# A chunked linear recurrence with a cosine-gated second part: one written order for all engines, the back substitution between block transposes, weights in small steps

## The chip, the cores and the metric

The kernel runs on one core of a Trainium2 chip. The metric is the device time of one execution in microseconds, the median of several runs. The engines of the core are TensorE (PE, with PEld for its weight loads), VectorE (DVE), ScalarE (ACT), GpSimd (POOL) and SyncE (SP, which here only issues DMAs). Each works through its own queue in order and waits on semaphores for the others.

## The reference

```python
# r, k, v, w, a, b: (batch 4, heads 8, seq 768, dim 40) float32
state = zeros(B, H, D, D)
for t in range(S):
    y[:, :, t] = einsum('bhd,bhde->bhe', rt, state)
    Sa = einsum('bhde,bhe->bhd', state, at)
    state = state * wt[:, :, None, :] - einsum('bhd,bhe->bhde', Sa, bt) \
            + einsum('bhd,bhe->bhde', vt, kt)
x = y.transpose(0, 2, 1, 3).reshape(3072, 320)
h = x @ w_in            # 320 x 2048, float64 in memory
out = (h * cos(h)) @ w_out   # 2048 x 320, float64 in memory
```

## The kernel before

The sequence is cut into 24 chunks of 32 steps. All four batches and eight heads of a chunk are worked on at once. Inside a chunk the recurrence is a triangular system, so each chunk needs the inverse of a 32 x 32 triangular matrix per head and batch. One DVE back substitution (`inv_step`, 31 steps of two operations each) gives the inverses of four chunks together, 128 of them, one per partition.

The work comes in segments that each use one tile `at` of PSUM, a pool of two buffers:

- `p1_w`, `p1_a` (once per chunk), `p1_b`, `p1_n` prepare two chunks: transposes of `w` (PSUM tile `wT`), running products on DVE (`wp`), their reciprocals (`rw`), scaled `a` and `b`, and the triangular matrices `nt`. They reach the layout of the back substitution over DRAM (`nd`, then `u`), and the inverses come back over DRAM too (`rd`, then `rt`).
- `p2_v`, `p2_k`, `p2_g` prepare one chunk ahead (tiles `vT`, `kT`, `gram`).
- `ch_t`, `ch_q`, `ch_x`, `ch_s`, `ch_z` (tiles `sT`, `qps`, `x0ps`, `sps`, `dps`) carry the state through the chunk. `ch_z` takes both buffers of `at`. Its four additions into the state `qz` and four into `yt` run on DVE, the four decays of `qz` on POOL. `ch_t` of the next chunk transposes `qz`.
- `yt` goes to DRAM (`xd`) and comes back as token columns `xT`.

The second part takes two chunks as one token group `g` and the 2048 columns in four blocks `j`. Each of the 48 pairs is four pieces: `first_a` and `first_b` (PSUM tiles `ph`, one buffer pair, with the rounding, Abs and Sin on ACT and DVE that give `gT`), and two `second` pieces of the pair before (tiles `po`). That makes 192 pieces. They are strewn between the segments by the counter `due`, 7.71 to a chunk from chunk 2 on; a piece of group `g` is allowed from chunk `2g + 2`.

The weights are float64. `rounded` turns the words into float32 with five DVE and two ACT operations per block, its DMAs issued from the ACT queue.

PE's order is the written one (`manual_schedule(engines={PE})`). On DVE, ACT, POOL and SP a list scheduler sets the order, so that an operation can pass others that are written ahead of it.

Of the kernel before, what the change touches and what calls it, by code (L numbers as in the profile page):

```python
# [9 lines left out]
F32 = mybir.dt.float32  # L10
# [10 lines left out]
def kernel(  # L21
# [11 lines left out]
):  # L33

# [70 lines left out]
    nat = {n: kept(f"nat_{n}", [P, H, DP], 2, 1.0, padding, nc.vector) for n in "w"}  # L105
    nat |= {n: kept(f"nat_{n}", [P, H, DP], 2, 0.0, padding) for n in "ab"}
    nat |= {n: kept(f"nat_{n}", [P, H, D], 1) for n in "kvr"}
# [9 lines left out]
    def load(c, names, via=nc.sync):  # L117
        for n in names:
            for i in range(B):
                via.dma_start(  # L120
                    nat[n][c % len(nat[n])][blk[i], :, :D],
                    src[n][i, :, c * C : (c + 1) * C, :].rearrange("h t d -> t h d"),
                )

    load(0, "w")
    load(1, "w")
    load(0, "a", nc.scalar)
    load(1, "a", nc.scalar)
    load(0, "b")
    load(1, "b")  # L130


    ident = kept("ident", [P, P])[0]
    make_identity(nc, ident)
# [9 lines left out]
    w0 = kept("w0", [P, 4 * B, C], 1, 0.0, on=nc.vector)[0]  # L144
    w1 = kept("w1", [P, 4 * B, C], 1, 0.0, on=nc.vector)[0]
    bn_b = kept("bn", [P, H, DP], 7, 0.0, padding)
    kn_b = kept("kn", [P, H, DP], 2, 0.0, padding)

    w_in_sb = const.tile([P, 2, DFF], F32, tag="w_in", name="w_in_sb")
    w_in_tail = const.tile([P, NF // 4, 2, P], F32, tag="w_in_tail", name="w_in_tail")
    w_out_sb = const.tile([P, NF, DM], F32, tag="w_out", name="w_out_sb")
# [5 lines left out]
    def rounded(dst, src, by, by_sb):  # L159


        n, wid = dst.shape[0], dst.shape[-1]
        words = sb2.tile([P, 512, 2], I32, tag="gT", name="words")[:n, :wid]
        for rows, part in src:
            nc.scalar.dma_start(words[rows].rearrange("p n w -> p (n w)"), part.bitcast(I32))
        lo, hi = words[:, :, 0], words[:, :, 1]
        mant = sb3.tile([P, 512], I32, tag="turns", name="mant")[:n, :wid]
        expo = sb2.tile([P, 512], I32, tag="expo", name="expo")[:n, :wid]
        frac = mant.bitcast(F32)
        nc.vector.tensor_scalar(  # L170
            expo, hi, 20, 0x7FF, ALU.logical_shift_right, ALU.bitwise_and
        )
        nc.scalar.activation(expo, expo, ACTF.Relu, bias=to_bits[:n], scale=2.0**23)
        nc.vector.tensor_scalar(mant, hi, 0xFFFFF, None, ALU.bitwise_and)
# [489 lines left out]
```

## Time and profile before

| | us |
|---|---|
| median of 3 runs (1079.9 to 1084.45) | 1080.34 |
| profiled execution | 1084.64 |
| its span | 1082.9 |
| PE busy | 820.3 (76%) |
| PE weight loads busy | 628.6 (58%) |
| DVE busy | 505.2 (47%) |
| ACT busy | 355.8 (33%) |
| POOL busy | 179.0 (17%) |
| mean granted TensorE clock | 0.884 |

The 40 slices of the page show three stages: some 100 us in which DVE is the busy engine and PE hardly works, a long middle with PE at 70 to 90%, and a last stretch of some 60 us with PE at 90% and more. In the chain that ended last PE has 54% of the span, DVE 20%, ACT 11% and DMA 8%. The costliest groups are the matmuls into `po` (249.2 us) and `ph` (208.9 and 56.7 us).

### The profile page before, as it was taken

Reading aid. Unit: us, or ns where it says so; the run is one execution under the profiler, and the core shown is the slowest. Engines: PE = TensorE matmul, PEld = TensorE weight load, DVE = VectorE, ACT = ScalarE, POOL = GpSimd, SP = SyncE. Lnnn points to the kernel's source line nnn. Section 1 sums busy time; section 2 is a strip of 40 time slices with the busy share of each in tenths; the row PEclk is TensorE's granted clock in tenths of the full one; section 3 lists DMA queues with packets and bytes.
Section 4 is the critical chain, followed back from the end, with each engine's and each line's share of the span. In section 5 each row is a group of like instructions: output and inputs, shape, how many; then the busy total and the mean of one; then the engine's idle time right before and its main releaser. Section 6 shows DMA issues by size and latency. Waiting matters only on the chain.

```text
span 1082.9 us, 36890 instructions
## 1 busy us (share of the span) xinstructions
PE 820.3 (76%) x16472; PEld 628.6 (58%) x16472; DVE 505.2 (47%) x1112; ACT 355.8 (33%) x679; POOL 179.0 (17%) x352
## 2 busy tenths in 40 slices
PE   4221366856679698788879879878987979999998
PEld 3110355644567576566667667656766757667775
DVE  6888124484452465251557263385255383233221
ACT  2341111422423242322243343224432424234343
POOL 4110123011120201120211120212022021111000
PEclk9999995877798798887898889889899989899999
DMA  5662432325124223124223123223241223200000
GB/s 114 147 159 40 83 62 55 38 57 137 35 50 62 52 46 72 34 44 59 49 47 78 37 57 55 54 48 67 40 82 25 47 57 56 46 15 10 21 26 12
DMA packets 235518, 61.65 MB, mean 57 GB/s; under 512 B 209504, under 2 KB 229472, under 8 KB 235360
## 3 DMA queue, kind: packets, MB, share of 16 engines
q1 hardware_dynamic: 229088, 48.48, 24.8%
q10 hardware_dynamic: 6272, 10.82, 3.5%
q8 instruction: 129, 2.11, 0.8%
q14 instruction: 29, 0.24, 0.1%
HBM read 45.09 MB, written 14.16 MB: 55 GB/s over the span
## 4 chain that ended last, share of the span: by engine, by line
PE 54%; DVE 20%; ACT 11%; DMA 8%; issue 4%; POOL 2%; SPq 1%; ACTq 0%; DVEq 0%; POOLq 0%
PE ph L97 20%; PE po L97 16%; DVE inv_tmp L309 3%; DVE inv L313 3%; PE gram L97 3%; DMA words<-in_moe_w_in_dram 3%; DVE rw L251 3%; ACT turns L531 3%; DMA words<-in_moe_w_out_dram 3%; PE x0ps L97 3%; ACT turns L530 3%; DVE wp L235 2%; PE vT L216 2%; PE qps L97 2%; PE sT L386 2%
## 5 line engine op out<-in xcount | busy, mean ns | idle before, releaser
L97 PE MATMUL po<-w_out_sb,gT 128*128 128x320 f32 x768 | 249.2, 476 | 0.3 <-issue 0.3
L97 PE MATMUL ph<-xT,w_in_sb 128*128 128x256 f32 x768 | 208.9, 426 | 20.3 <-DVE w_in_sb L182 9.5
L97 PEld LDWEIGHTS po<-w_out_sb,gT 128*128 128x128 f32 x768 | 154.1, 209 | 67.9 <-issue 23.6
L97 PEld LDWEIGHTS ph<-xT,w_in_sb 128*128 128x128 f32 x768 | 160.3, 215 | 50.7 <-DVE w_in_sb L182 10.4
L529 DVE SCALAR_TENSOR_TENSOR turns<-turns,ph 128x512 f32<-128x512 f32 x96 | 61.6, 682 | 212.1 <-ACT turns L528 212.0
L528 ACT ACTIVATE turns<-ph,rnd 128x512 f32<-128x512 f32 x96 | 60.9, 684 | 176.8 <-PE ph L97 176.8
L532 DVE TENSOR_TENSOR gT<-ph,turns 128x512 f32<-128x512 f32 x96 | 65.8, 690 | 59.8 <-ACT turns L531 59.6
L309 DVE TENSOR_TENSOR inv_tmp<-u,inv 128x31 f32<-128x31 f32 (+15 forms) x186 | 69.2, 372 | 5.5
L313 DVE TENSOR_TENSOR inv<-inv,inv_tmp 128x31 f32<-128x31 f32 (+15 forms) x186 | 68.4, 368 | 5.7
L531 ACT ACTIVATE turns<-turns,half_pi 128x512 f32<-128x512 f32 x96 | 68.7, 723 | 1.8
L97 PE MATMUL gram<-aT,kT 40*32 40x32 f32 x1536 | 20.0, 222 | 64.8 <-DVE yt L482 49.6
L530 ACT ACTIVATE turns<-turns 128x512 f32<-128x512 f32 x96 | 59.3, 625 | 10.6 <-DVE turns L529 10.6
L97 PEld LDWEIGHTS gram<-aT,kT 40*32 40x32 f32 x1536 | 17.2, 124 | 69.4 <-issue 52.0
L97 PE MATMUL ph<-xT,w_in_tail 64*128 64x256 f32 x384 | 56.7, 415 | 0.0
L378 ACT COPY vvm<-gram 128x256 f32<-128x256 f32 x24 | 8.9, 372 | 137.9 <-DVE vvm L374 137.9
L251 DVE RECIPROCAL rw<-wn 128x320 f32<-128x320 f32 x24 | 51.5, 2148 | 5.0 <-PE wn L216 5.0
L476 POOL TENSOR_TENSOR qz<-qz,wc 128x160 f32<-128x160 f32 x92 | 40.0, 462 | 68.5 <-DVE qz L475 68.5
L328 POOL TENSOR_TENSOR kn<-nat_k,rw 128x320 f32<-128x320 f32 x24 | 21.2, 882 | 177.0 <-PE dps L97 170.1
L216 PE MATMUL bT<-ident,bn 128*128 128x128 f32 x96 | 22.4, 377 | 33.3 <-POOL bn L256 11.2
L264 ACT COPY bT<-bT 128x512 f32<-128x512 f32 x24 | 14.1, 586 | 101.5 <-PE bT L216 101.3
L239 POOL COPY wx<-wp 128x496 f32<-128x496 f32 x24 | 15.0, 626 | 193.2 <-DVE wp L235 190.8
L97 PEld LDWEIGHTS ph<-xT,w_in_tail 64*128 64x128 f32 x384 | 34.6, 195 | 20.0 <-issue 17.2
(93 smaller groups left out, 1096.9 us busy)
## 6 DMA issues: line engine op xcount, KB each, us to landing
words<-in_moe_w_out_dram ACTq DMA_DIRECT2D x16, 320.0 KB
words<-in_moe_w_in_dram ACTq DMA_DIRECT2D x8, 512.0 KB
nat_w<-in_w_dram SPq DMA_DIRECT2D x96, 40.0 KB
nat_b<-in_b_dram SPq DMA_DIRECT2D x96, 40.0 KB
nat_k<-in_k_dram SPq DMA_DIRECT2D x96, 40.0 KB
nat_v<-in_v_dram SPq DMA_DIRECT2D x96, 40.0 KB
nat_r<-in_r_dram SPq DMA_DIRECT2D x96, 40.0 KB
xd<-yt SPq DMA_DIRECT2D x48, 80.0 KB
```

Source lines behind the costliest of these rows:

```text
L97: nc.tensor.matmul(o, lhsT=lhsT, rhs=rhs, start=start, stop=stop, skip_group_check=True)
L216: nc.tensor.transpose(ps[:, i * P : (i + 1) * P], x[:, 2 * i : 2 * i + 2].rearrange("p e d -> p (e d)"), ident)
L235: nc.vector.tensor_tensor_scan(flat(wp), flat(w0), flat(w1), 0.0, ALU.mult, ALU.add)
L251: nc.vector.reciprocal(rw, unpad(ps[:, 0].rearrange("p (h d) -> p h d", h=H)))
L309: nc.vector.tensor_tensor(tmp, u[:, :j, j : j + 1].to_broadcast([P, j, C - j]), x[:, j : j + 1, j:].to_broadcast([P, j, C - j]), ALU.mult,)
L313: nc.vector.tensor_tensor(x[:, :j, j:], x[:, :j, j:], tmp, ALU.subtract)
L476: nc.gpsimd.tensor_tensor(z, z, wc.rearrange("p (f m b) -> p f m b", f=2, m=2)[:, :, :, bb] .unsqueeze(3).to_broadcast([P, 2, 2, D]), ALU. ...
L528: nc.scalar.activation(n, u, ACTF.Identity, bias=rnd, scale=1.0)
L529: nc.vector.scalar_tensor_tensor(n, n, -ROUND, u, ALU.add, ALU.subtract)
L530: nc.scalar.activation(n, n, ACTF.Abs)
L531: nc.scalar.activation(n, n, ACTF.Sin, bias=half_pi, scale=-2.0 * math.pi)
L532: nc.vector.tensor_tensor(G["gT", j][:, 2 * e : 2 * e + 2].rearrange("p f t -> p (f t)"), u, n, ALU.mult)
```

## The change

- `manual_schedule()` without engines: all engines follow the written order. The code hands out operations by hand for that: `later(n, work)` puts work n steps behind, `step` runs a segment or piece and then what has come due, and adds up to `of_inv` back substitution steps and `of_w` weight steps behind each segment or piece (1, in every fourth chunk 2, and 4 or 3).
- The order of segments within a chunk is new, one piece count of 8 per chunk from 2.4 on replaces 7.71 from 2 on.
- `nt` and the inverses go through DVE block transposes (`nc.vector.transpose`, 32 x 32) instead of DRAM. `inv_step` itself is unchanged. The 33 steps of one back substitution all lie in the chunk whose number is 3 modulo 4.
- The running product reads PSUM: the column copies `w0` on ACT go, a `memset` of every 32nd column in PSUM comes, and one tile `wb` replaces `wp` and `wx` (no POOL copy of 496 columns).
- The inputs of chunks 0 to 3 have landing places of their own at first; those of 2 and 3 lie in parts of `w_in_sb` and `w_out_sb` that the weights fill later. All are fetched at the start.
- Weights come in 36 blocks (28 before: `w_in` in halves of 256 columns), fetched from the POOL queue, three ahead, converted in chunks 0 to 3.
- `ph`'s products are issued one step after the rest of `first_b`.

```diff
-    w0 = kept("w0", [P, 4 * B, C], 1, 0.0, on=nc.vector)[0]
+    w1 = kept("w1", [P, 4 * B, C], 2, 0.0, on=nc.vector)
...
+        def fetch():
+            t["words"] = sb3.tile([P, DM, 2], I32, tag="words", name="words")[:n, :wid]
+            for rows, part in src:
+                nc.gpsimd.dma_start(
...
+    def step(work, of_inv=0, of_w=0):
+        before = list(waiting)
+        work()
+        for w in before:
+            w[0] -= 1
+            if w[0] == 0:
+                waiting.remove(w)
+                w[1]()
+        for steps, n in ((inv_steps, of_inv), (w_steps, of_w)):
+            for _ in range(min(n, len(steps))):
+                steps.pop(0)()
...
-            nc.scalar.copy(w0[:, :, 1:], b4(ps[:, i])[:, :, 1:])
...
+        nc.vector.memset(ps[:, :, ::C], 0.0)
+        for i in range(2):
+            wb = ring.tile([P, 4 * P + 1], F32, tag="wb", name="wb")
+            nc.vector.tensor_tensor_scan(wb[:, 1:], ps[:, i], flat(w1[i]), 0.0, ALU.mult, ALU.add)
...
-        nc.sync.dma_start(nd.rearrange("p h t -> p (h t)"), nt.rearrange("p c e n -> p (c e n)"))
...
+        nc.vector.transpose(
+            G["u"].rearrange("p (s t) -> p t s", s=C), G["nt"].rearrange("p h t -> p t h")
+        )
...
-        nc.sync.dma_start(rd.rearrange("p s t -> p (s t)"), G["inv"])
...
+        nc.vector.transpose(
+            rt.rearrange("p c h t -> p t (c h)"), G["inv"].rearrange("p (s t) -> p t s", s=C)
+        )
...
-    with tc.manual_schedule(engines={mybir.EngineType.PE}):
+    with tc.manual_schedule():
...
+        START, done = 2.4, 0
...
+            if c == 0:
+                segs = [x, v, extra[0], s, k, extra[1], z, g, *extra[2:]]
+            elif len(extra) == 3:
+                segs = [t, v, q, k, x, extra[0], s, g, z, *extra[1:]]
+            elif len(extra) == 2:
+                segs = [t, v, q, k, x, g, s, extra[0], z, extra[1]]
+            else:
+                segs = [t, v, q, k, x, g, s, z]
...
+            fill = (1 + (c % 4 == 3), 4 if c < 2 else 3)
+            for i, seg in enumerate(segs):
+                step(seg, *fill)
+                due = (c + (i + 1) / n - START) * 8
...
+                    step(pieces[done][1], *fill)
...
+                if c % 4 == 2 and len(extra) == 2 and seg is extra[1]:
+                    inv_steps.extend(inverse(q0))
```

On PE, around `ch_z` of a chunk in the middle. Before:

```order
L97 MATMUL sps<-x_6813,rt 32x72 x32
L216 MATMUL kT<-ident_128,kn_161 128x128 x4
L97 MATMUL ph<-xT,w_in_sb 128x256 x4
L97 MATMUL ph<-xT,w_in_tail 128x256 x4
L97 MATMUL dps<-vvm_101,kn_163 64x72 x32
L97 MATMUL dps<-sm,bn_155 64x72 x32
L97 MATMUL gram<-aT,kT 32x32 x32
L97 MATMUL gram<-rT,vT 32x32 x32
L97 MATMUL po<-w_out_sb,gT 128x320 x8
L386 MATMUL sT<-ident_128,qz_102 128x128 x8
```

After:

```order
L101 MATMUL gram<-aT,kT 32x32 x32
L101 MATMUL gram<-rT,vT 32x32 x32
L101 MATMUL po<-w_out_sb,gT 128x320 x4
L101 MATMUL sps<-x_5274,rt 32x72 x32
L101 MATMUL ph<-xT,w_in_sb 128x256 x4
L270 MATMUL bT<-ident_84,bn_202 128x128 x4
L270 MATMUL bT<-ident_84,bn_204 128x128 x4
L101 MATMUL ph<-xT,w_in_sb 128x256 x4
L101 MATMUL ph<-xT,w_in_tail 128x256 x4
L101 MATMUL dps<-vvm_114,kn_206 64x72 x32
L101 MATMUL dps<-sm,bn_194 64x72 x32
L101 MATMUL nps<-aT,bT 32x32 x64
```

`gram` no longer follows `dps`; it stands two segments ahead of it, and behind `dps` comes a `p1` segment or a piece.

On DVE, in a chunk that carries the back substitution (`inv_tmp`, `inv`). Before, where steps run in a row until an operation with a due time of its own comes:

```order
L309 TENSOR_TENSOR inv_tmp<-u,inv 128x135
L313 TENSOR_TENSOR inv<-inv,inv_tmp 128x27x5
L309 TENSOR_TENSOR inv_tmp<-u,inv 128x156
L313 TENSOR_TENSOR inv<-inv,inv_tmp 128x26x6
L427 COPY x_4232<-x0ps 128x288
L309 TENSOR_TENSOR inv_tmp<-u,inv 128x175
L313 TENSOR_TENSOR inv<-inv,inv_tmp 128x25x7
```

After, near the end of the fourth chunk:

```order
L560 TENSOR_TENSOR yt<-dps,qz_116 128x4x32
L381 TENSOR_TENSOR inv_tmp<-u,inv 128x112
L385 TENSOR_TENSOR inv<-inv,inv_tmp 128x4x28
L381 TENSOR_TENSOR inv_tmp<-u,inv 128x87
L385 TENSOR_TENSOR inv<-inv,inv_tmp 128x3x29
L616 SCALAR_TENSOR_TENSOR turns<-turns,ph 128x512 x2
L381 TENSOR_TENSOR inv_tmp<-u,inv 128x60
L385 TENSOR_TENSOR inv<-inv,inv_tmp 128x2x30
L381 TENSOR_TENSOR inv_tmp<-u,inv 128x31
L385 TENSOR_TENSOR inv<-inv,inv_tmp 128x31
L327 RECIPROCAL rw<-wn 128x320
L329 TENSOR_TENSOR aT<-wn,wb 128x512
```

Two steps (four operations) stand behind every segment and piece, in one chunk of four.

On SP, between the write of `xd` and the read of `xT`. Before:

```order
L493 DMA xd<-yt 40x4x128 x2
L120 DMA nat_b_91<-in_b_dram 32x8x40 x2
L500 DMA xT<-xd 128x2x128
L502 DMA xT<-xd 64x128 x2
L120 DMA nat_b_91<-in_b_dram 32x8x40
```

After:

```order
L574 DMA xd<-yt 40x4x128 x2
L149 DMA nat_k<-in_k_dram 32x8x40 x4
L149 DMA nat_v<-in_v_dram 32x8x40 x4
L149 DMA nat_r<-in_r_dram 32x8x40 x4
L584 DMA xT<-xd 128x2x128
L586 DMA xT<-xd 64x128 x2
```

Twelve loads of a coming chunk now stand between the two.

## Rows read from the trace of the kernel before

**Rows 1.** Stretches: bounds, length, busy us of the engines, clock, DMA share, GB/s.

```profile
core 0: us, PE busy (x) PEld busy (x) DVE busy (x) ACT busy (x) POOL busy (x), PEclk, DMA share, GB/s
921.25:1012.39 91.14, 84.50 (x1828) 64.58 (x1835) 25.52 (x62) 34.46 (x67) 12.21 (x21) 0.93 0.11 27
301.73:921.25 619.52, 522.81 (x10901) 400.57 (x10908) 292.89 (x642) 209.19 (x406) 113.57 (x211) 0.87 0.29 53
96.05:301.73 205.68, 123.75 (x2717) 96.68 (x2717) 92.56 (x219) 53.16 (x103) 33.41 (x62) 0.81 0.32 62
...
1012.39:1082.90 70.51, 65.18 (x584) 47.96 (x584) 19.04 (x33) 26.67 (x45) 1.27 (x1) 0.99 0.05 15
```

**Rows 2.** PE in order of time, around `gram` behind `dps`: start, us, idle before.

```profile
568.56 0.82 PE L97 MATMUL gram<-aT,kT 40*32 40x32 f32 x60 [5.92 <-DVE yt L482]
...
572.29 5.53 PE L97 MATMUL po<-w_out_sb,gT 128*128 128x320 f32 x13 [0.30 <-issue]
```

**Rows 3.** Chain that ended last, pieces back to back at its end.

```profile
1041.69 4.50 PE po L97 x16
1046.20 4.52 PE ph L97 x24
```

**Rows 4.** PE in order of time, a chunk's segments with little idle time.

```profile
611.82 1.04 PE L386 MATMUL sT<-ident,qz 128*128 128x128 f32 x8
...
613.56 1.89 PE L97 MATMUL ph<-xT,w_in_sb 128*128 128x256 f32 x8
615.38 1.14 PE L97 MATMUL qps<-rT,s 40*64 40x32 f32 x64
616.45 0.66 PE L216 MATMUL kT<-ident,kn 128*128 128x128 f32 x4
617.78 0.72 PE L97 MATMUL gram<-aT,kT 40*32 40x32 f32 x62 [0.67 <-ACT kT L349]
...
619.00 1.99 PE L97 MATMUL ph<-xT,w_in_sb 128*128 128x256 f32 x8
...
624.34 0.88 PE L97 MATMUL x0ps<-vvm,ag 32*32 32x72 f32 x64
...
625.97 1.09 PE L216 MATMUL wT<-ident,nat_w 128*128 128x128 f32 x8
626.90 2.32 PE L97 MATMUL po<-w_out_sb,gT 128*128 128x320 f32 x8
629.15 0.88 PE L97 MATMUL sps<-x,rt 32*32 32x72 f32 x64
...
638.20 0.91 PE L97 MATMUL dps<-sm,bn 32*64 32x72 f32 x62
```

**Rows 5.** DVE groups by line: forms, count, busy us, mean ns, idle before.

```profile
L309 DVE TENSOR_TENSOR inv_tmp<-u,inv 128x31 f32<-128x31 f32 (+15 forms) x186 | 69.2, 372 | 5.5
L313 DVE TENSOR_TENSOR inv<-inv,inv_tmp 128x31 f32<-128x31 f32 (+15 forms) x186 | 68.4, 368 | 5.7
...
L529 DVE SCALAR_TENSOR_TENSOR turns<-turns,ph 128x512 f32<-128x512 f32 x96 | 61.6, 682 | 212.1 <-ACT turns L528 212.0
L251 DVE RECIPROCAL rw<-wn 128x320 f32<-128x320 f32 x24 | 51.5, 2148 | 5.0 <-PE wn L216 5.0
L235 DVE TENSOR_TENSOR_SCAN wp<-w,w 128x512 f32<-128x512 f32 x24 | 29.4, 1223 | 15.6 <-ACT w L233 15.6
```

**Rows 6.** DVE in order of time: first operations of two weight blocks in a row.

```profile
51.28 0.33 DVE L170 TENSOR_SCALAR expo<-words 128x320 int32<-128x320 int32 x1 [0.37 <-DMA words<-in_moe_w_out_dram]
...
53.47 0.32 DVE L170 TENSOR_SCALAR expo<-words 128x320 int32<-128x320 int32 x1
```

**Rows 7.** PE in order of time before the first back substitution.

```profile
52.49 1.09 PE L216 MATMUL wn<-ident,nat_a 128*128 128x128 f32 x4 [18.80 <-DMA nat_a<-in_a_dram]
...
61.89 1.64 PE L97 MATMUL nps<-aT,bT 40*32 40x32 f32 x128
```

**Rows 8.** PE in order of time, `ch_z` of chunk 1 and the first piece.

```profile
175.09 1.30 PE L97 MATMUL dps<-sm,bn 32*64 32x72 f32 x60
...
186.97 1.62 PE L97 MATMUL ph<-xT,w_in_sb 128*128 128x256 f32 x3 [3.18 <-DMA xT<-xd]
```

More of the change, by code (lines that the diff above doesn't have):

```diff
@@ L162, in rounded @@
         n, wid = dst.shape[0], dst.shape[-1]
[L163 to L172, printed above, removed]
@@ L210, in at @@
+        return work
     def at(name):
@@ L223, with later @@
     G = {}
+    waiting = []
+    inv_steps, w_steps = [], []
+    def later(steps, work):
+        waiting.append([steps, work])
+    def step(work, of_inv=0, of_w=0):
[9 more added lines that the diff above has]
+                steps.pop(0)()
     def p1_w(c):
@@ L489, in ch_z, with tokens @@
         )
+        later(2, lambda: tokens(c, yt))
+    def tokens(c, yt):
         xd = dram.tile([DM, P], F32, tag="xd", name="xd")
@@ new lines, in p1, with p2, last, main @@
+        return [lambda: p1_w(c), lambda: p1_a(c), last_a, lambda: p1_b(c), lambda: p1_n(c)]
+    def p2(c):
+        def last():
+            p2_g(c)
+            if c + 1 < NCH:
+                later(1, lambda: p2_in(c + 1))
+        return [lambda: p2_v(c), lambda: p2_k(c), last]
+    def main(c):
+        def last():
+            ch_z(c)
+            if c + 2 < NCH:
+                later(1, lambda: p2_kn(c + 2))
+        return [lambda: ch_t(c), lambda: ch_q(c), lambda: ch_x(c), lambda: ch_s(c), last]
@@ new lines @@
+    with tc.manual_schedule():
+        first, other = p1(0), p1(2)
+        w_work = weights()
+        for seg in first[:3]:
+            step(seg)
+        step(other[0])
+        for i in range(3):
+            w_work[i][0]()
+        step(first[3])
+        step(first[4])
+        step(other[1])
+        step(other[2])
+        p2_in(0)
+        p2_kn(0)
+        v, k, g = p2(0)
+        for seg in (v, k, g, *other[3:]):
+            step(seg)
+        for work in inverse(0):
+            work()
+        w_ends = []
+        for n, (_, parts) in enumerate(w_work):
+            w_steps.extend(parts)
+            if n + 3 < len(w_work):
+                w_steps.append(w_work[n + 3][0])
+            w_ends.append(len(w_steps))
+        w_all = len(w_steps)
+        p2_kn(1)
+        START, done = 2.4, 0
@@ L604 @@
         for c in range(NCH):
+            t, q, x, s, z = main(c)
+            v, k, g = p2(c + 1) if c + 1 < NCH else [lambda: None] * 3
             q0 = c - c % 4 + 4
[L606 to L613 removed]
@@ L638 @@
+        for g, work, j in pieces[done:]:
+            if g == NCH // 2 - 1 and j == 0:
+                while waiting:
+                    step(lambda: None)
+            step(work)
+        while waiting:
+            step(lambda: None)
 _INS = ["r", "k", "v", "w", "a", "b", "moe_w_in", "moe_w_out"]
```

321 lines of the change are left out of this document (168 added, 153 removed).

## The prediction, made before the changed kernel was run

> **What bounds the kernel now.** I read the 40 slices of the page first, then cut the span into stretches at the first products of `ch_x` in chunks 0, 4, 20 and 23 [rows 1]. Up to chunk 0 there are 96.05 us, with almost no second part; chunks 0 to 3 take 205.68, chunks 4 to 19 take 619.52 (38.7 a chunk), chunks 20 to 22 take 91.14 (30.4), the end 70.51. The reader should compare PE's busy time with the length: 60% in the second stretch, 84% in the third, 93% in the fourth. So the long middle is close to PE-bound, and what can be won there is PE's idle time and the clock, 0.87 against 0.93 or 0.99 later. Next I read PE in order of time. A typical hole is `gram` right behind `dps`: it waits 5.92 us for DVE's `yt`, and the next 13 products into `po` then take 5.53 us [rows 2], whereas 16 take 4.50 in the packed end [rows 3]. The clock falls after a hole, so a hole costs more than its length. DVE's groups came last [rows 5]: its 186 + 186 back substitution operations, 137.6 us for six, are 22.9 us each.
>
> **A chunk on PE without waits.** From start to start [rows 4]: `sT` with `vT` 1.74, `qps` 1.07, `kT` 0.66, `gram` 1.22, `x0ps` 1.63, `sps` about 0.81, `dps` two halves of about 0.82, 1.64: 8.8 us. Four pieces take 4.50 + 4.52 = 9.02 [rows 3], so eight take 18.0. The `p1` segments, four for two chunks, lie between 0.93 [rows 4] and 1.64 [rows 7], at the mean 5.2 for two, 2.6 a chunk. Sum 29.4 at full clock. I add 1.1 for a clock of 0.93 as in the fourth stretch: 30.5.
>
> **Before chunk 0.** Before the change the last `nps` ends at 61.89 + 1.64 = 63.5, and 18.80 us of that were `wn` waiting for `nat_a` [rows 7]. With all inputs fetched at the start that wait should go: 44.7, say 46 with `p2` of chunk 0 ahead of it. Then come the back substitution, 22.9, and block transposes on DVE of 1024 elements a partition on both sides. No row shows one. Nearest are operations that pass 512 elements: 0.68 (`turns`) and 1.22 (the scan) [rows 5]; twice these are the bounds, 1.4 and 2.4. I take 1.6, near the lower, as a transpose is no running sum; 3.2 for the two. So the first inverses are there at 46 + 26 = 72. The round trip over DRAM goes with it. On the page "Vector Engine (DVE) Microarchitecture Reference", section 3.8, the Trainium skill says that the transpose mode keeps up one element per cycle and lane; by that a transpose would be an estimate of 1.1 us, and the whole some 6 us less for twelve of them. No row bears on it yet.
>
> **Chunks 0 to 3.** DVE has 36 weight blocks to convert; one of 320 columns takes 2.19 from start to start [rows 6]. 16 such and 20 smaller ones of about 2.0 (256 columns, a guess between the proportion, 1.75, and no saving) are 75 us. Its other work in a chunk is (292.89 − 4 × 22.9) / 16 = 12.6 [rows 1, 5]; four chunks less some 18 missing pieces (0.68 each, as `turns` [rows 5]) are 38. The second back substitution with transposes is 26. Sum 139, and about 5 us a chunk in which DVE waits for PE in turn: 159. DVE bounds this stage, as PE has at most 123.75 to do in it [rows 1]. From 72 that leads to 231, and some 10 us lie between the start of a chunk and its `ch_x`: chunk 4's comes at **241**, against 301.73. Gain 61. The weights must be converted anyway; the gain is that they fill what was idle DVE time (92.56 of 205.68 busy) instead of standing ahead of it.
>
> **Chunks 4 to 19.** `gram` now stands ahead of `dps` and asks for nothing that `ch_z` makes, so the 5.92 goes. What is late next is DVE's strict queue. PE's `ch_q` needs the additions into `qz` first, `ch_s` the copies of `x0ps`, and these now wait behind whatever is written ahead of them: one step, 0.74 us, per segment in the light chunks, two in the fourth. Even chunks: 30.5 + 1 for such waits, 31.5. Chunk 1 of four, with `rw` (2.15) and the scan ahead of what `ch_t` and `ch_s` ask for, three waits of about 1: 33.5. Chunk 3 of four carries everything: 12.6 + 3.4 (two more `rw` and scans than the mean chunk [rows 5]) + 26.1 for the back substitution = 42.1 on DVE, more than PE's 30.5; DVE is the bound there, and I add 5 for its own waits at hand-overs: 47. With 1.5 for a late `xT` four chunks are 31.5 + 33.5 + 31.5 + 47 + 1.5 = 145. The order supports that DVE can't spread it: every step stands in that chunk. Three times 145, and 136 for chunks 16 to 19 (chunk 19 has a back substitution, but no `p1` is left: 26.1 + 12.6 − 3.4 = 35.3 on DVE, and 3 of waits, 38), are 571: chunk 20's `ch_x` at **812**, against 921.25. Gain 48.5.
>
> **Chunks 20 to 22.** 29.4 − 2.6 = 26.8, + 1.1 + 1.2 of waits: 29.1 each, 87 against 91.14.
>
> **The end.** Between the end of a `dps` and the first piece of its tokens lie 10.6 us (176.39 to 186.97) [rows 8], and SP now has twelve loads between write and read, though in the last chunk there are none left. At chunk 23 the written order leaves only two pieces, 4.5 us [rows 3], to cover them: 6.1 us of PE wait, and at the low clock 6.8 instead of 4.5 for the 16 products into `po` after it (5.53 / 13 each [rows 2]), 2.3. Two pieces fewer are left than before (−4.5), and the chunk itself is 2 shorter: 70.51 + 8.4 − 6.5 = 72.
>
> **Sum.** 812 + 87 + 72 = 971 of span, against 1082.9. Outside the span lie 1084.64 − 1082.9 = 1.74 us: 973 for a profiled execution like the one shown. That one was 4.3 above the median of the runs, so 969, rounded to **970**.
>
> **Rivals.**
> 1. *The fourth chunk costs like the others.* If DVE's waits fall together with the back substitution steps, or the transposes are short, chunk 3 of four takes 34 to 36: three times 12 and once 7 are about 43 less, and 5 in chunk 3 beside, **922** (900 to 935). For it: DVE was only 47% busy in the third stretch (292.89 of 619.52). Against it: the 42.1 are busy time, which no order shortens below.
> 2. *The gain is smaller: PE's clock stays at 0.87 and each hand-over costs a little.* With a mean chunk of 37.5 instead of 35.7, and 2 to 3 us in each of chunks 0 to 3, the time is **1000 to 1010** (990 to 1045). For it: the third stretch ran at 0.87 with 16% of idle time, and the written order has as many hand-overs as before.
> 3. *The weights come late.* They are now fetched by DMAs from the POOL queue, of which no row here shows one; two of the five DVE operations of a block are of 0.33 us with one source [rows 6]. In-order DVE would stop at each late block with the state's operations behind it. Bounds: nothing (three blocks ahead), and 36 blocks that each come about 1 to 1.4 us late, 36 to 50. That gives **1005 to 1020**. The Trainium skill, "SBUF — State Buffer", section "SBUF: two separate sides", has a rule against this change: while DVE runs an operation in a two-port mode, GpSimd can't write the descriptors of its DMAs, so that these seem blocked by DVE. By it up to 36 × 0.66 = 24 us of descriptor writing would be put off, most of it hidden by the three blocks ahead. Nothing in the trace of before can show it.
> 4. *The convoy: slower than before.* The list scheduler let an operation pass one whose input was late; now each engine stops with all behind it. If every segment or piece, some 18 in a chunk including `p1`, makes PE wait once for a DVE or ACT that itself stood waiting, the price is 18 × 20 chunks × the wait. The gain of 110 is gone at 110 / 360 = 0.31 us a hand-over; at 0.5 it is **1150** (1095 to 1160). For it: `gram` waited 0.67 for a plain `kT` copy [rows 4], so single waits of this size do exist. Against it: pieces stand between almost all dependent segments, each over 2 us long, and a hand-over shorter than a piece is covered.
> 5. *The order changes nothing that counts*, within 0.5% of 1080.34 (about what a measurement of this kernel can tell from no change): all gains of the start eaten by a DVE-bound middle. That needs 110 us of such waits exactly.
>
> **How the numbers follow.** Forecast 970 (own range 935 to 990) 0.55; rival 1 0.12; rival 2 0.18; rival 3 0.06; rival 4 0.07; rival 5 0.02. Faster: 0.55 + 0.12 + 0.18 + 0.06 = 0.91; same 0.02; slower 0.07. For 8 times in 10 the range takes in the forecast's own range, most of rival 1, and rivals 2 and 3 up to 1040: 918 to 1040. The bounds of a transpose (12 × 0.2 below or 12 × 0.8 above) move the sum by 2 to 10 us and lie inside.
>
> **What the profile of after would show.** Right: `ch_x` of chunk 4 near 241 and of chunk 20 near 812; `gram` no more waiting for `yt`; every fourth chunk 10 us or more longer than its neighbours with DVE over 85% busy in it; PE's clock at 0.9 or more between; a transpose between 1.4 and 2.4 us; a wait of some 6 us ahead of the first piece of the last group. Wrong: DVE under 85% in the fourth chunk while that chunk is still long (then it is hand-overs, rival 2 or 4); DVE stopped at the weights' first operation with a DMA as what ended the wait (rival 3); PE waits of half a microsecond at most segments of every chunk (rival 4); or fourth chunks like the others (rival 1). If the inputs of the start come no earlier, since they share the queues with more loads, the 18.80 stays and the forecast is 989.

## The result, and the profile after

| | before | after |
|---|---|---|
| median, us | 1080.66 | 978.43 |
| runs, lowest to highest | 4, 1079.9 to 1084.45 | 4, 975.64 to 981.53 |
| span of the profiled execution | 1082.9 | 973.6 |
| PE busy, us | 820.3 | 782.4 |
| DVE busy, us | 505.2 | 535.9 |

The ratio is 0.9048 (95% interval 0.9013 to 0.9083). The forecast was 970, its range 918 to 1040; for the span it had 971, and the profiled execution, the quickest of the four, has 973.6. Kernels below are compared by their ratio to the kernel before on the same chip, since that kernel's own median lay between 1072.9 and 1080.7 from chip to chip.

These stretches of after have the bounds of [rows 1]: the first `ch_x` of chunks 0, 4, 20 and 23. The columns are bounds, length, busy us (count) of the engines, granted clock, DMA share, GB/s.

```profile
core 0: us, PE busy (x) PEld busy (x) DVE busy (x) ACT busy (x) POOL busy (x), PEclk, DMA share, GB/s
0.00:44.01 44.01, 21.63 (x460) 18.01 (x461) 18.78 (x24) 5.99 (x13) 17.07 (x58) 0.78 0.60 98
44.01:256.56 212.55, 121.35 (x2602) 95.62 (x2596) 173.42 (x405) 76.65 (x153) 52.64 (x98) 0.66 0.35 81
256.56:826.27 569.71, 501.92 (x11049) 386.28 (x11048) 301.24 (x657) 212.53 (x399) 102.55 (x194) 0.95 0.22 42
826.27:909.46 83.19, 81.28 (x1826) 61.67 (x1825) 26.00 (x63) 36.60 (x69) 12.41 (x21) 1.00 0.12 30
909.46:973.60 64.14, 56.27 (x545) 41.34 (x544) 16.47 (x29) 23.57 (x40) 1.27 (x1) 1.00 0.06 17
```

The reader should set them beside [rows 1]. Up to chunk 4 it was 301.73 us and is 256.56: 45.2 won. Chunks 4 to 19 took 619.52 and take 569.71: 49.8. Chunks 20 to 22 give 8.0, the end 6.4. PE's work is nearly the same; in the long middle its clock went from 0.87 to 0.95 and its idle time from 96.7 to 67.8.

What is won up to chunk 4 is won ahead of the first `sps`, the first product that needs the inverses: it starts at 75.22 us and not at 123.54. From there to chunk 4 the two kernels take 181.3 and 178.2 us. Before, 21 of the 28 weight blocks were converted ahead of that point. Now 34 of the 36 stand behind it, DVE is busy 144.8 us in that stretch and not 81.4, and it is only 3 us longer.

What PE waits for in chunks 4 to 19, by line and releaser (us in total, times, the longest):

```profile
PE gram L101 <- DVE wb L311: 16.9, 7, 4.4
PE nps L101 <- DVE yt L560: 10.3, 7, 1.5
PE ph L101 <- DMA xT<-xd: 9.9, 5, 6.6
PE sT L464 <- DVE aT L329: 7.7, 7, 1.6
```

`gram` no longer waits for `yt`. In the same chunks of the kernel before that was the largest wait of PE:

```profile
PE gram L97 <- DVE yt L482: 31.4, 7, 6.7
```

It now waits for the scan `wb`, up to 4.4 us, and that only where `p1_w` stands ahead of it. `nps`, which in every second chunk now follows `dps`, waits for `yt` instead, up to 1.5 us.

The fourth chunk: from the transpose ahead of the back substitution to the end of the one behind it, then the stretch up to the next one (windows as above).

```profile
343.17:390.31 47.14, 39.18 (x658) 30.10 (x658) 40.09 (x91) 13.60 (x26) 7.78 (x16) 0.86 0.19 38
390.31:485.81 95.50, 87.59 (x2113) 67.61 (x2112) 37.40 (x77) 39.67 (x74) 18.36 (x35) 0.98 0.26 49
```

DVE is busy 85% of the first and 39% of the second. From `ch_x` to `ch_x` chunks 7, 11 and 15 take 41.7, 42.6 and 42.7 us, their neighbours 31 to 36. DVE is busy 81%, 79% and 78% of these three, and chunk 19, with DVE at 62%, takes 41.4 as well. Chunks 7 and 19:

```profile
356.08:397.74 41.66, 33.70 (x639) 26.15 (x637) 33.68 (x69) 12.45 (x24) 8.46 (x17) 0.88 0.18 34
784.82:826.27 41.45, 31.73 (x613) 23.71 (x612) 25.83 (x65) 11.99 (x23) 5.22 (x9) 0.88 0.12 23
```

### The profile page after: what moved, and what is told of

It reads as the page before. It is cut to its first block, busy times and chain, and to the rows that moved or that the text cites. A ratio compares the mean times of both kernels' runs of the same rounds, so it can differ in the third digit from the quotient of the medians.

```text
span 973.6 us, 36928 instructions
## 1 busy us (share of the span) xinstructions
PE 782.4 (80%) x16472; PEld 602.9 (62%) x16472; DVE 535.9 (55%) x1178; ACT 355.3 (36%) x671; POOL 185.9 (19%) x372
## 4 chain that ended last, share of the span: by engine, by line
PE 49%; DVE 23%; ACT 10%; issue 6%; SPq 5%; DMA 4%; POOL 2%; POOLq 0%; ACTq 0%; DVEq 0%
PE ph L101 21%; PE po L101 13%; SPq L149 5%; DVE inv_tmp L381 4%; DVE inv L385 4%; ACT turns L614 2%; DVE wb L311 2%; PE qps L101 2%; PE gram L101 2%; DVE turns L616 2%; ACT turns L619 2%; ACT turns L618 2%; DMA xT<-xd 2%; PE sT L464 2%; PE dps L101 2%
## 5 line engine op out<-in xcount | busy, mean ns | idle before, releaser
L101 PE MATMUL po<-w_out_sb,gT 128*128 128x320 f32 x768 | 237.1, 455 | 1.0 <-issue 1.0
L101 PE MATMUL ph<-xT,w_in_sb 128*128 128x256 f32 x768 | 203.3, 412 | 22.6 <-DMA xT<-xd 14.3
L101 PEld LDWEIGHTS ph<-xT,w_in_sb 128*128 128x128 f32 x768 | 149.6, 204 | 48.3 <-issue 24.1
L101 PEld LDWEIGHTS po<-w_out_sb,gT 128*128 128x128 f32 x768 | 144.1, 197 | 56.7 <-issue 9.2
L554 POOL TENSOR_TENSOR qz<-qz,wc 128x160 f32<-128x160 f32 x92 | 41.4, 466 | 332.2 <-DVE qz L553 331.6
L468 ACT COPY s<-sT 128x512 f32<-128x512 f32 x46 | 24.7, 588 | 58.5 <-PE sT L464 58.5
L200 ACT ACTIVATE expo<-expo,to_bits 128x256 int32<-128x256 int32 (+1 forms) x36 | 19.2, 533 | 72.7 <-DVE expo L197 72.7
L522 ACT COPY sm<-sps 128x160 f32<-128x160 f32 x48 | 14.0, 291 | 77.8 <-DVE sm L526 43.4
L270 PE MATMUL wT<-ident,nat_w 128*128 128x128 f32 x88 | 14.6, 315 | 34.2 <-DVE x L505 23.7
L313 POOL COPY wc<-wb 128x16 f32<-128x16 f32 x24 | 5.4, 225 | 186.0 <-DVE wb L311 186.0
L101 PE MATMUL dps<-vvm,kn 32*64 32x72 f32 x1536 | 27.3, 255 | 16.8 <-ACT vvm L456 8.4
L101 PE MATMUL gram<-aT,kT 40*32 40x32 f32 x1536 | 19.2, 211 | 26.8 <-DVE wb L311 23.1
```

What stands on the lines that cost most here:

```text
L101: nc.tensor.matmul(o, lhsT=lhsT, rhs=rhs, start=start, stop=stop, skip_group_check=True)
L468: nc.scalar.copy(G["s"][:, 4 * i : 4 * i + 4].rearrange("p i e -> p (i e)"), ps[:, i])
L554: nc.gpsimd.tensor_tensor(z, z, wc.rearrange("p (f m b) -> p f m b", f=2, m=2)[:, :, :, bb] .unsqueeze(3).to_broadcast([P, 2, 2, D]), ALU. ...
```

## The experiments

**Is it DVE's work that makes the fourth chunk long?** The 31 steps are left out there, the transposes stay.

```diff
-                    inv_steps.extend(inverse(q0))
+                    inv_steps.extend([inv_start, lambda: inv_end(q0)])
```

> The changed kernel without the 31 subtraction steps of the back substitution in chunks 3, 7, 11, 15 and 19 (the two transposes stay; so the inverses are not computed there; the first one, ahead of chunk 0, stays). In the changed kernel the stretch from the first x0ps of chunk 7 to that of chunk 8 is 41.7 us against 33 to 34 of its neighbours, 11 and 15 likewise 42.6 and 42.7, 19 is 41.5. Theory A (the forecast's: DVE's work bounds the fourth chunk): these fall to 33 to 34, and 3 as well by some 8, in all about 42 less: 936. Rival B (the fourth chunk is long because PE waits at hand-overs: gram for the PSUM buffer that the scan of p1_w still reads, dps for vvm, sT for aT, and the low clock after that): the scan and the reciprocals are still there, each fourth chunk falls by 3 at most: 963 or more.

Measured: 939.04, ratio 0.8705 (0.8671 to 0.8740). Chunk 7:

```profile
347.69:381.51 33.82, 30.65 (x639) 23.80 (x637) 16.09 (x28) 12.45 (x24) 8.15 (x17) 1.00 0.21 41
```

33.8 us and full clock, as its neighbours. The difference in ratio, 0.0343 of 1080, is 37 us, 7 to 8 on average for each of five back substitutions that keep DVE busy 23 us each. Theory A holds for what costs; it does not say yet that DVE's share alone is the bound.

**Or the buffer that the scan holds?** The copy is on ACT again.

```diff
-        nc.vector.memset(ps[:, :, ::C], 0.0)
...
+        for i in range(2):
+            nc.scalar.copy(b4(wbs[i][:, 1:])[:, :, 1:], b4(ps[:, i])[:, :, 1:])
...
-            nc.vector.tensor_tensor_scan(wb[:, 1:], ps[:, i], flat(w1[i]), 0.0, ALU.mult, ALU.add)
+            nc.vector.memset(wb[:, 1::C], 0.0)
+            nc.vector.tensor_tensor_scan(wb[:, 1:], wb[:, 1:], flat(w1[i]), 0.0, ALU.mult, ALU.add)
```

> The changed kernel with one part undone: ACT copies the transposed w out of PSUM (into wb, in which the scan then runs in place), so that the PSUM buffer is free after two copies of some 0.6 us and not after DVE's scans, which stand behind four steps of the back substitution. In the changed kernel gram waits 4.4 us for that in chunks 3, 7, 11 and 15, and the clock is low after it. Theory A (DVE's work bounds the fourth chunk): DVE has the same work, the wait moves to a later segment, the time stays: 973 to 981. Rival B (the held buffer makes the chunk long): four times 4.4 and some 1.5 of low clock go, 24 less: 952 to 958.

Measured: 975.78, ratio 0.9058 (0.9025 to 0.9090): no difference. PE's largest wait in chunks 4 to 19 of this kernel:

```profile
PE dps L101 <- DVE sm L529: 22.1, 4, 6.6
```

The 16.9 at `gram` went, and at `dps`, which had waited 3.1 for `sm` in all, there are 22.1 now: 6.2 to 6.6 in each of chunks 7, 11 and 15, 3.0 in 19. Freeing the buffer behind the backlogged DVE only moved the wait to the next thing that DVE owes. The buffer isn't the cause, the queue of DVE is.

**Does it help to spread the steps?** One behind each segment and piece of the fourth chunk, the rest in the next one.

```diff
-            if c % 4 == 0:
-                while inv_steps:
-                    inv_steps.pop(0)()
-            fill = (1 + (c % 4 == 3), 4 if c < 2 else 3)
+            fill = (1, 4 if c < 2 else 3)
             for i, seg in enumerate(segs):
+                if c % 4 == 0 and seg is s:
+                    while inv_steps:
+                        inv_steps.pop(0)()
```

> The changed kernel with one step of the back substitution, not two, behind each segment and piece of the fourth chunk, and the rest of them in the next chunk ahead of ch_s, where the inverses are first asked for. No work is left out. Theory A (DVE's busy time bounds the fourth chunk, which the run without the steps supports with 40 us): the fourth chunk falls from 42 to 34 or 35, the next one stays at 33 to 34: 940 to 955. Rival B (what costs is each step that stands ahead of an operation of the state, wherever it stands): the fourth chunk gains 4 to 5 and the next one loses as much: 970 to 982.

Measured: 974.68, ratio 0.9089 (0.9046 to 0.9133): no difference, as theory B had it. Chunks 7 and 8:

```profile
350.55:386.52 35.97, 30.62 (x639) 23.72 (x637) 30.76 (x64) 12.45 (x24) 8.99 (x17) 1.00 0.20 37
386.52:428.05 41.53, 33.53 (x749) 25.51 (x748) 15.42 (x41) 14.17 (x27) 5.23 (x9) 0.88 0.22 45
```

Chunk 7 came down to 36.0 with DVE at 86%, chunk 8 went up from 34.0 to 41.5 with DVE at 37%. A chunk with an idle DVE as long as one with a full one is against the plain form of theory A: there PE waits for single results. One row of PE in chunk 8 shows which:

```profile
397.85 1.25 PE L101 MATMUL sps<-x,rt 32*32 32x72 f32 x64 [3.56 <-DVE rt L389]
```

The rushed last steps and the transpose stood in front of `sps`, 3.56 us of wait, and behind it the clock was 0.87 up to 410 us and 0.81 in the rest of the chunk; up to `sps` it was 0.99.

**Spread without the rush**, together with the copy on ACT: 28 steps in the fourth chunk (two and one in turn), 5 in the next.

```diff
...
-                step(seg, *fill)
...
+                step(seg, 1 + (c % 4 == 3 and k2 % 2), fill_w)
...
```

> Two edits of the changed kernel at once, with no work left out: in the fourth chunk of four one and two back substitution steps in turn behind segments and pieces (28 of 33), the other 5 one by one in the next chunk, so that the last transpose is done ahead of ch_s without a rush; and ACT copies the transposed w out of PSUM ahead of the scan. In the run with the steps spread evenly the fourth chunk took 36 instead of 42 us, but the next one 37 to 41 instead of 33 to 34, since sps waited 3.6 us for the rushed rest and the clock was low after it; in the run with the copy alone gram's wait for the scan was gone and the time the same. Theory A (it is the sum of DVE's work over the fourth and the next chunk; without a rush the two take 70 to 72 instead of 75): five times 4 and 4 in front, 955 to 962. Theory B (a step ahead of an operation of the state costs the same wherever it stands): 970 to 980.

Measured: 967.98, ratio 0.8987 (0.8941 to 0.9033): the time lies between the two theories, by its ratio some 6 us below after, which is theory B's range, with intervals that overlap. Chunks 7 and 8 take 40.0 and 37.0, together 77.0 against 75.7 in after; the pairs 11 and 12, 15 and 16 are 2.2 and 0.7 shorter (74.0 and 74.7). So the sum over a pair hardly depends on where the steps stand: within what was tried, 23 us of DVE work cost 7 to 8 us wherever they are put. Why they cost that much where DVE has idle time was not settled; chunk 8 above shows one way, a single late result.

**The place of `gram`.** It is the next segment behind `dps` again, from chunk 1 on. In every second chunk the edit moves more than that: `p1_b` (`extra[0]`), which stood between `ch_s` and `ch_z`, goes behind `gram`.

```diff
...
             elif len(extra) == 2:
-                segs = [t, v, q, k, x, g, s, extra[0], z, extra[1]]
+                segs = [t, v, q, k, x, s, z, g, extra[0], extra[1]]
             else:
-                segs = [t, v, q, k, x, g, s, z]
+                segs = [t, v, q, k, x, s, z, g]
```

> The changed kernel with one part undone: gram of the next chunk stands right behind dps again from chunk 1 on (and behind it the p1 segments), not two segments ahead. Theory A (the 5.9 us for which PE waited at that place is the price, as the prediction put it): 3 to 5 us a chunk with the low clock after it, 20 chunks: 1035 to 1075. Rival B (DVE's four additions into yt are now at the head of its queue, and a piece may follow, so that the wait is 1 to 2 us): 995 to 1015. Rival C (the order of segments is worth nothing beside the rest): 973 to 985.

Measured: 1026.03, ratio 0.9552 (0.9491 to 0.9613). This form works on `r` and `v` of a wrong chunk, since their copies stand behind the loads of the next ones, and a wait for these can't be told from one for `gram`. So it was made again with the copies of `r` and `v` ahead of the loads.

```diff
...
-                later(1, lambda: p2_kn(c + 2))
+                later(1, lambda: (p2_in(c + 2), p2_kn(c + 2)))
...
```

> As the run with gram behind dps, but the copies of r and v for the chunk after next are written ahead of the loads that replace them, one step behind dps. In the first form two pieces could stand between dps and gram; the copies then came behind the loads and took the r and v of the wrong chunk, and vT waited for these loads: its 1026 hold a wait that has nothing to do with gram. Theory A (the place of gram was worth the 5.9 us holes): still above 1010. Theory B (DVE's additions are at the head of its queue now, a wait of 1 to 3 us at gram stays, with the low clock after it): 990 to 1010. Theory C (all of the 48 in the first form were the loads): 973 to 985.

Measured: 1008.77, ratio 0.9351 (0.9286 to 0.9416): at the upper edge of theory B's range. The edit costs 0.0303 of 1080, 33 us. PE's waits in chunks 4 to 19 of this kernel, which take 609.0 us:

```profile
PE bT L270 <- ACT bT L340: 33.3, 8, 4.2
PE dps L101 <- DVE wb L311: 16.9, 7, 4.4
PE dps L101 <- DVE sm L526: 13.4, 8, 3.8
PE sT L464 <- DVE aT L329: 8.7, 7, 2.0
```

`gram` isn't in the list, so theory B's wait isn't there either. The waits are at its neighbours. `dps` has the 16.9 for the scan that `gram` had in after, and, as it follows `sps` without `gram` between, it stands for `sm`. The 33.3 at `bT` are eight waits of 4.16, one in each of chunks 4, 6 and so on to 18, such as

```profile
350.29 1.08 PE L270 MATMUL bT<-ident,bn 128*128 128x128 f32 x4 [4.16 <-ACT bT L340]
```

There `p1_b` stands right behind a piece, and ACT does that piece's operations before the copy which the second half of `bT` waits for. These chunks are the ones that got longer, by 3.5 to 7.4 us each and 42 in all. The odd chunks 5 to 19, where `gram` alone changed its place, are 3 us shorter in all. So what the 33 us buy is the place of `p1_b`, and that of `gram` is not shown to be worth anything: behind `dps` it waits at most 1.4 us for `yt` in this kernel (in chunks 0 and 1, where no piece falls between), and not the 5.92 of [rows 2].

**Who orders the other engines.** Only PE in written order, as before the change:

```diff
-    with tc.manual_schedule():
+    with tc.manual_schedule(engines={mybir.EngineType.PE}):
```

> The changed kernel with only PE in written order; the other engines' order comes from the list scheduler, as in the kernel before. Theory A (the gain is from the early start, the weights in DVE's idle time and the place of gram; who orders the other engines is worth little): 965 to 995. Rival C (written order costs by convoys, the scheduler could let the state's operations pass the fill): 940 to 960. Rival D (the written order is itself most of the gain, since the scheduler puts fill ahead of what the chain asks for): over 1010.

Measured: 983.52, ratio 0.9111 (0.9060 to 0.9161): theory A, with an interval that overlaps the one of after. Its stretches:

```profile
55.55:250.67 195.12, 115.06 (x2604) 91.64 (x2597) 143.46 (x351) 66.79 (x132) 54.08 (x90) 0.68 0.33 73
250.67:820.29 569.62, 502.56 (x11050) 387.81 (x11049) 297.19 (x657) 210.13 (x399) 101.77 (x192) 0.93 0.21 42
820.29:914.49 94.20, 86.07 (x1826) 63.26 (x1825) 26.29 (x63) 35.67 (x68) 12.31 (x21) 0.96 0.09 25
```

The middle is 569.62 against 569.71: the same time with the scheduler's order as with the written one. The scheduler is 11.5 later at chunk 0, 17.4 quicker through the weights, and 16 slower from chunk 20 on. In its order chunks 7, 11 and 15 take 36.7, 36.5 and 35.6 us and the others 31 to 39: the back substitution is spread, and the middle is as long.

**The transposes.** Both layouts go over DRAM again.

```diff
-        nc.vector.transpose(
-            G["u"].rearrange("p (s t) -> p t s", s=C), G["nt"].rearrange("p h t -> p t h")
-        )
...
+        nc.sync.dma_start(nd.rearrange("p h t -> p (h t)"), G["nt"].rearrange("p h t -> p (h t)"))
+        for g in range(4):
+            nc.sync.dma_start(
+                G["u"][blk[g]].rearrange("h (s t) -> h s t", s=C), nd[blk[g]].rearrange("s h t -> h s t")
+            )
...
```

> The changed kernel with one part undone: nt and the inverses change their layout over DRAM again (one write and four reads each on SP's queue) in place of the two block transposes on DVE, which take 2.1 and 1.9 us. In the kernel before, 22.4 us lay between the start of the last nps and the first back substitution step, and 15.3 between the last step and sps; in the changed kernel 4.6 and 4.7. Theory A (the transposes carry a good part of the gain at the start, and in written order a late trip stops DVE with the state's operations behind it): about 18 + 10 us at the start, and 5 to 15 in each of the five later back substitutions: 1020 to 1075. Rival B (with few other transfers in flight a trip takes 4 to 6 us and most of it is covered in the middle): 985 to 1005.

Measured: 1096.27, ratio 1.0201 (1.0136 to 1.0266), beyond both expectations and slower than the kernel before. DVE's first step in chunk 7:

```profile
391.44 0.21 DVE L385 TENSOR_TENSOR inv_tmp<-u,inv 128x31 f32<-128x31 f32 x1 [18.01 <-DMA u<-nd]
```

DVE stands for 18.0 us, with the copies, `sm` and the additions of the state behind it, and chunk 7 takes 66.1 us and not 41.7. The other four late ones wait 11.0 to 19.3. In the kernel before, under the list scheduler, DVE never stood idle for `u`; in written order it stops the core. The order and the transposes depend on each other, so their shares can't be added up.

**The start.** The inputs of chunks 2 and 3 share the places of 0 and 1 again, and their `p1_w` goes behind `p1_n` of 0 and 1.

```diff
...
-    for c in range(4):
+    for c in range(2):
         load(c, "a", nc.scalar)
...
+        for n in "wab":
+            load(2, n)
+            load(3, n)
...
```

> The changed kernel with one part undone: the inputs w, a, b of chunks 2 and 3 share the two landing places of chunks 0 and 1, as in the kernel before, and are fetched once p1 of chunks 0 and 1 has read those. In the changed kernel the first block transpose starts at 44.9 us. Theory A (the wait for nat_a, 18.8 us in the kernel before, went by the own landing places): the wait comes back with 10 to 19 us, the first transpose starts at 55 to 64, and as nothing can catch it up (DVE is full in chunks 0 to 3), the time rises by the same: 988 to 998. Rival E (the start was gained by the order and by the transposes in place of the trip over DRAM; the loads are in time anyway): the first transpose within 4 us of 44.9, the time within 5 us of 978.

Measured: 981.54, ratio 0.9116 (0.9076 to 0.9155). The first transpose starts at 44.88 us, as in after: rival E. The time is 3 us above that of after, by ratio 7, with intervals that overlap. So the 18.80 us at `nat_a` [rows 7] did not come from the shared places. Where from, the kernel before without its weights (set to a constant) was to tell:

```diff
-                rounded(dst, src, by, by_sb)
+                nc.gpsimd.memset(dst, 0.01)
```

> The kernel before without fetching and converting the weights (POOL sets them to a constant). The question is what the 18.8 us of PE waiting for nat_a of chunk 2 came from, since the changed kernel with the landing places as before lost only 3 us. Theory F (the 24 early weight transfers: SP stood for 26.6 us of the first 125 behind transfers of words): the wait falls below 4 us, and the last nps ahead of the back substitution ends by 48 and not at 63.5. Rival G (the loads of chunks 2 and 3 must wait until p1 of chunks 0 and 1 has read the shared places, or stand behind the trip of nt on SP): the wait stays above 10. The time itself loses the weights' 80 us of DVE work, which in the kernel before stood partly in front of the back substitution: 1000 to 1045.

Measured: 1024.96, ratio 0.9582 (0.9521 to 0.9642). The rows of PE that answer to [rows 7]:

```profile
31.90 1.11 PE L216 MATMUL wn<-ident,nat_a 128*128 128x128 f32 x4 [3.77 <-DMA nat_a<-in_a_dram]
...
39.86 1.64 PE L97 MATMUL nps<-aT,bT 40*32 40x32 f32 x128
```

The wait is 3.77 and the last `nps` starts at 39.86 in place of 61.89: theory F. In the kernel before, SP, which issues the loads, had this (SP's waits in its first 125 us):

```profile
SPq L120 <- DMA words<-in_moe_w_in_dram: 14.7, 4, 8.5
...
SPq L120 <- DMA words<-in_moe_w_out_dram: 11.9, 7, 2.8
```

So the 18.80 came from the weights, and by these rows from their transfers, behind which SP stood with the inputs. The run leaves out their conversion too and doesn't separate the two. In after only three blocks are fetched ahead. That this freed the start was not tried by itself; what did not free it are the landing places and the transposes, since the last `nps` ahead of the back substitution starts at 42.36 without the first and at 41.97 without the second, and at 42.39 in after. The written order of the other engines has a part in it: with only PE in written order that `nps` starts at 53.96.

**The weights.** The steps are turned by one, so that ACT's step is done between two slots.

```diff
         w_all = len(w_steps)
+        for _ in range(2):
+            w_steps.pop(0)()
```

> The changed kernel with the weight steps turned by one: a slot holds the product of the block before and then exponent and mantissa of the next one, in place of one whole block. In the changed kernel DVE waits 13 us in chunks 0 to 3, 0.3 to 0.6 a block, for ACT's step between mantissa and product, which then is done in the slot before. The stage from the first x0ps to that of chunk 4 took 212.6 us. Theory A (these waits are a part of why the weights cost 93 us and not the 75 of the forecast): half to all of the 13 goes, as DVE is full there: 966 to 973. Rival (DVE's waits there are covered; PE's chain through the segments sets the stage): 975 to 982.

Measured: 978.52, ratio 0.9096 (0.9046 to 0.9146): the rival. Some waits of DVE between 44 and 257 us:

```profile
DVE sm L526 <- ACT sm L522: 6.6, 7, 3.5
...
DVE x L505 <- ACT x L504: 3.6, 4, 1.0
DVE w_out_sb L219 <- ACT mant L210: 2.9, 8, 0.9
...
DVE w_in_sb L219 <- ACT mant L210: 1.7, 6, 0.3
...
DVE w_in_tail L219 <- ACT mant L210: 0.8, 3, 0.3
```

The waits for `mant`, 13.1 in after, are 5.4, and the ones for `sm` and `x`, 1.4 and 1.3 in after, grew instead; the stage is as long.

**The tokens.** On top of the spread steps and the copy, the trip of the tokens is written one step earlier and ahead of the twelve loads.

```diff
...
-            later(2, lambda: load(c + 1, "kvr"))
+            later(2 if c < 3 else 4, lambda: load(c + 1, "kvr"))
...
-        later(2, lambda: tokens(c, yt))
+        later(1, lambda: tokens(c, yt))
...
```

> The run with 28 and 5 back substitution steps and the scan's copy on ACT, and beside it the tokens' trip over DRAM written one step earlier and ahead of the loads of the next k, v and r on SP's queue (in the changed kernel these twelve loads stand between the write of xd and the read of xT). In that run PE waited 9.8 us for xT in chunks 4 to 19, 6.8 of it once, and 2.7 more at the last group. Theory A (a wait for a transfer in front of a PE-bound stretch is lost time): the xT waits fall under 3 us in all and the time falls by 6 to 9: 959 to 962. Rival (the wait is covered by what follows, which waits for DVE anyway): 965 to 969.

Measured: 957.46, ratio 0.8913 (0.8877 to 0.8950), the best kernel of this study. Its waits for `xT` from chunk 4 to the end, then those of the same kernel without this edit:

```profile
PE ph L101 <- DMA xT<-xd: 6.8, 3, 2.7
```

```profile
PE ph L101 <- DMA xT<-xd: 14.4, 6, 6.8
```

7.6 us less wait and 0.0074 of 1080, 8 us, less time, with intervals that just overlap, though the waits did not fall under 3: of what was tried, the only wait of PE whose removal was paid back.

## Why the prediction held, point by point

**Start: right in size, wrong in its reason.** The first inverses were forecast for 72 and are there at 72.5. That sum rested on "with all inputs fetched at the start that wait should go". The wait went, but the experiment with two places shows that it goes without the fetch too, and the kernel before without its weights that it came from these. The forecast had [rows 7] name a DMA as the releaser and took the nearest edit for the cure; that the size held is luck. What the start won shows at the first `sps`, from both ends: the kernel before without its weights has it at 89.41 and not at 123.54, and after with the trips over DRAM put back has it at 88.72 and not at 75.22. So by these two runs some 34 us of the 48 are the weights, which no longer stand ahead of it, and some 13.5 are the transposes. The written order keeps the weights behind: with only PE in written order, DVE starts on two thirds of them ahead, and the first `sps` starts at 104.63. Yet that kernel is at chunk 4 by 250.67, 6 us before after, since fewer weights are left then; on which side of the first `sps` they stand is not by itself what was won.

**A transpose: mis-sized.** Taken at 1.6, it is 2.07 ahead of and 1.91 behind the back substitution, inside its bounds of 1.4 and 2.4.

```profile
44.91 2.07 DVE L373 STREAM_TRANSPOSE u<-nt 128x1024 f32<-128x1024 f32 x1
...
70.57 1.91 DVE L389 STREAM_TRANSPOSE rt<-inv 128x1024 f32<-128x1024 f32 x1
```

For 1024 elements that is 2.0 ns an element. The estimate of 1.1 us from the Trainium skill's page "Vector Engine (DVE) Microarchitecture Reference", section 3.8, does not agree with it.

**Chunks 0 to 3: the step that fell short.** Forecast 241 for chunk 4's `ch_x`, measured 256.6. The stretch from the inverses on is

```profile
72.40:256.56 184.16, 117.80 (x2524) 92.94 (x2524) 147.34 (x340) 76.25 (x152) 50.95 (x95) 0.68 0.37 88
```

DVE is busy 147.3 in it, where the sum had 139, and idle 36.8, where it had 30 ("about 5 us a chunk" of waits and 10 up to `ch_x`). So both terms were short, by 8 and by 7. The 8 are work that the sum left out. It took four times DVE's mean chunk in chunks 4 to 19 of before, which has one `rw`, one scan and one `aT` a chunk; the first four chunks of after prepare six chunks. `rw` by itself, in this stretch of after and in chunks 4 to 19 of before (bounds, length, DVE busy, clock, DMA share, GB/s):

```profile
72.40:256.56 184.16, 12.87 (x6) 0.68 0.37 88
301.73:921.25 619.52, 34.37 (x16) 0.87 0.29 53
```

Two more of each, at 2.15, 1.17 and 0.63 us, are 7.9. The turned weight steps show that the waits aren't one that could be taken out: with `mant` out of the way, others filled the same time.

**Chunks 4 to 19: 571 forecast, 569.7 measured, by errors that cancel.** That is luck. The fourth chunk was to take 47 and takes 42, 14 us less for the three of them. The twelve light ones were to take 98 for three and take 99.5 to 102, 9 us more in all, and chunk 19 takes 41.4 and not 38. What a clock below full costs was taken too small: PE is busy 31.4 us a chunk (501.92 / 16) at 0.95, where the sum had 30.5 at 0.93; in chunks 20 to 22, at 1.00, it is busy 27.1 and the sum had 26.8. (The working counts four `p1` segments for two chunks where there are five; they take 2.7 us a chunk all the same, and the sum had 2.6.)

The 42.1 us of DVE were put into the chunk from `ch_x` to `ch_x`, but the back substitution begins 13 us ahead of that point (343.2 against 356.1), in an otherwise light stretch, so that chunk 7 holds 33.7 and not 42.1. That DVE's steps are what makes it long is shown by the run without them. That DVE "is the bound there" is wrong by the forecast's own sign, DVE under 85% in a fourth chunk that is still long: from `ch_x` to `ch_x` it is 78 to 81%, and 62% in chunk 19. Spread steps also cost the same in a chunk where DVE is 37% busy. So hand-overs between engines, the mechanism of rivals 2 and 4, have a part in its length.

`gram`'s hole went as told, but its new place is not shown to be the reason: behind `dps` again, in written order, it waits at most 1.4 us for `yt`, and the 33 us of that edit are `p1_b`'s. The traces point to the order of DVE. At the hole of [rows 2] `dps` ended at 562.65 and DVE began its additions 4.8 us later, behind back substitution steps and a piece's operations that the scheduler had put between; in after, in chunk 6, `dps` ends at 339.10 and they begin 0.4 us later. Before, then after:

```profile
567.47 0.32 DVE L475 TENSOR_TENSOR qz<-dps,qz 128x160 f32<-128x160 f32 x1
```

```profile
339.48 0.32 DVE L553 TENSOR_TENSOR qz<-dps,qz 128x160 f32<-128x160 f32 x1
```

This was not tried by itself.

**The end: 72 forecast, 64.1 measured.** After the last `dps`:

```profile
919.69 0.91 PE L101 MATMUL dps<-sm,bn 32*64 32x72 f32 x62
920.52 4.57 PE L101 MATMUL po<-w_out_sb,gT 128*128 128x320 f32 x16
927.82 2.40 PE L101 MATMUL ph<-xT,w_in_sb 128*128 128x256 f32 x10 [2.73 <-DMA xT<-xd]
```

The tokens' trip took 7.2 us, not the 10.6 of [rows 8]; that one was the first of all, and why it was longer no run shows. The wait is 2.7 and not 6.1, and the clock stays full after it, so the 2.3 for a low clock weren't due either. The other 2 us are PE's work: it fell from 65.18 to 56.27 us busy, by 8.9, where the sum had 6.5. Chunks 20 to 22 took 83.2 and not 87, at clock 1.00 and not 0.93.

**The rivals.** Chunks 7, 11 and 15 do not cost like the others (rival 1). The clock rose (rival 2). The weights weren't late (rival 3): in the whole stage DVE waited once for their DMAs,

```profile
DVE expo L197 <- DMA words<-in_moe_w_out_dram: 0.2, 1, 0.2
```

so the rule of the Trainium skill, "SBUF — State Buffer", section "SBUF: two separate sides", on DMAs from the GpSimd queue cost nothing that DVE waited for: with three blocks ahead a late descriptor would not be seen, and no run here shows one. The convoy (rival 4) isn't there as a whole, since the scheduler's order of the other engines gives the same middle; it is there in the small, in the waits that moved on when one was taken away, and in full where a late input meets the written order, as the trip over DRAM showed.

## What to carry to other kernels

Before a wait is taken out, ask what its releaser owes next: here, behind a backlogged engine that works in order, the wait moved on, and only work that was left out or a transfer that was started earlier was paid back. A written order needs inputs that are never late, so a layout change on the engine itself (2 us) was worth far more here than the trip over DRAM that it replaced. When an edit moves two segments, compare the chunks in which it moved both with those in which it moved one: a whole-kernel time gave `gram` a price that was `p1_b`'s. And a forecast that comes out right still wants its terms tested: here a term missing 15 us and terms 13 us too long met, and three of its causes, for the start, for the fourth chunk and for `gram`, did not hold as told.

## What the runs showed of the hardware that the forecast had not counted

In this trace DVE's back substitution steps, which read two SBUF operands, stretch where they meet POOL's operations on SBUF. In chunk 7, DVE and then POOL:

```profile
380.04 0.42 DVE L385 TENSOR_TENSOR inv<-inv,inv_tmp 128x112 f32<-128x112 f32 x1
380.49 1.20 DVE L381 TENSOR_TENSOR inv_tmp<-u,inv 128x87 f32<-128x87 f32 x1
381.73 0.80 DVE L385 TENSOR_TENSOR inv<-inv,inv_tmp 128x87 f32<-128x87 f32 x1
```

```profile
380.29 1.29 POOL L565 TENSOR_TENSOR yt<-yt,wb 128x512 f32<-128x512 f32 x1
381.55 0.87 POOL L409 TENSOR_TENSOR kn<-nat_k,rw 128x320 f32<-128x320 f32 x1
```

The same step takes 0.25 us for 87 elements when POOL is still (48.21 us in the same trace); here 1.20 and 0.80, each ending 0.1 us after POOL's operation. It is some 1.5 us at this place, and the same steps take 1.20 and 0.79 or 0.80 beside the same POOL operations in chunks 3, 11 and 15. Over all steps that overlap a POOL operation the trace adds up to some 10 us above the same steps without one, an estimate; what that costs in time was not tried.
